# Routing tail of a top-1 mixture of experts: second expert chosen after 8 of 12 token tiles, expert units placed between the last routing steps

## The chip, the cores and the metric

One NeuronCore of one Trainium2 chip (trn2), one launch, float32 inputs and output. The metric is the device time of that launch in microseconds (us); before the change it is 557.35 us, the median of 3 runs.

## The reference, cut to what matters

```python
def _attn_ref(q, k, v, n_global, n_local):      # B, H, S, D = 2, 8, 768, 64; n_global 8, n_local 96
    scores = (1.0 / sqrt(D)) * q @ k^T
    keep = is_global | is_local                  # columns below n_global, and the last n_local before the row
    scores = where(keep, scores + bias, -1e9)    # bias: -slope(head) * distance
    return softmax(scores) @ v

def _moe_ref(x, w_gate, w_local, w1, w2):        # D, E, F = 512, 8, 1024
    logits = x @ w_gate                          # [B, S, 8]
    local_gate = sigmoid(x @ w_local)
    for b in range(B):
        for s in range(S):
            fresh_e = argmax(logits[b, s])
            e = fresh_e if s == 0 or local_gate[b, s] < 0.5 else prev_e   # else: the expert of the token before
            prev_e = e
            out[b, s] = softmax(logits[b, s])[e] * (relu(x[b, s] @ w1[e]) @ w2[e])

def _moe2_ref(x, mu_k, mu_r, w_k, w_v, w_r):     # mixes each token with the one before it
    k = relu(xk @ w_k);  v = k * k @ w_v;  r = sigmoid(xr @ w_r)
    return r * v

reference: _moe2_ref(_moe_ref(_attn_ref(q, k, v)))
```

## The kernel before, in words

The 1536 tokens (2 batches of 768) are 12 **tiles** of 128 rows. Every float32 operand of the big products is split into a high and a low part of the faster float32r format, and a product is three matmuls: high by high, low by high, high by low (`mm3`, L624 to L626).

**Attention with routing inside it.** A loop over i = 0 to 24 (`NI` is 24) does half a tile of attention (4 heads) per step: scores (L750, L754), exponentials on ScalarE (L774), transposes of the probabilities on TensorE (L785, L787), copies out of PSUM (`pt`, L794 and L796), product with v (L810). When a tile is done its output X is scaled (`route_x`, L178) and its logits are taken (`route_lg`, L192). Two tiles make a routing **group**, and a group goes through a chain of short operations that hops between engines: logits on TensorE; maximum and argmax on VectorE (L198 to L222); transposes to one row on TensorE (L232); a copy on ScalarE (`br`, L235); a scan along the row on VectorE that resolves "the expert of the token before" (L243); back to columns on TensorE (L251); one-hot on VectorE (L256); running counts on TensorE (L265 to L271); positions on VectorE (L283 to L297). Then GpSimd scatters the rows of X by expert to DRAM (`scatter`, L275); at most 3 tiles X are held. The table `plan` (filled by `at`) says in which step of the loop each link of the chain of a group is issued: its logits go to step 2 g + 4 (g is the group's second tile).

**Early expert.** After 6 tiles the counts choose the first expert (`order_a`, `order_b`, `early_pick`), its weights `wraw` (w1 in chunks 0 to 3, w2 in chunks 4 to 7, 512 KB each, 4 buffers) are loaded on SyncE's queue and split: `whi` on ScalarE (some on VectorE), `wlo` = raw minus high on GpSimd (`w_lo1`, `w_lo`), 512 or 1024 columns at a time.

**Tail.** When attention ends, the last group (tiles 10 and 11) still has its whole chain to go. Into it the kernel places **units** of the first expert's first two tiles (`fill`, `F_`): a unit is the three matmuls of one 128-row slice of the product; a tile has 16 of them (8 of w1, 8 of w2) and three sets of four transposes. `TAILF` and `RANKF` say how many units stand after each link. At the chain's end all 12 tiles' counts are known, `ranks` orders the experts, and only then the weights of the second expert are loaded. The third tile of the first expert follows, then the experts 1 to 7 in order of their counts: 256 rows each, and 80 rows more for the second (`CAPS`, `TILES`, `LAST`). If an expert has more rows than its capacity, a flag sends the kernel through `general`, which computes everything anew.

**After the experts** the rows are gathered back and the third part of the reference runs in 6 blocks of 256 tokens (L1262 to L1302).

All of it is scheduled by hand: each engine runs its instructions in the order in which the program issues them, and waits are on semaphores. Pools of buffers are released after their last reader.

## Time and profile before

| | |
|---|---|
| three timed runs | 558.14, 556.28, 557.35 us; median 557.35 |
| the profiled execution | 553.79 us, of which 551.8 us lie between first and last instruction |
| TensorE (PE) | busy 522.6 us, 95% |
| weight loads of TensorE (PEld) | busy 444.1 us, 80% |
| VectorE (DVE) | busy 349.7 us, 63% |
| ScalarE (ACT) | busy 258.4 us, 47% |
| GpSimd (POOL) | busy 117.5 us, 21% |
| mean granted clock of TensorE | 0.975 of full speed |
| chain of work that ended last | PE 74%, DVE 12%, DMA 7% |

All times of rows are counted from the start of the span. The profile gives each engine's busy time, for each idle stretch the instruction that ended it (written `[idle <-releaser]`), and the clock that TensorE was granted, as a share of its full speed; 0.50 means the lower of its two levels, 1.2 GHz, and 1.00 the upper, 2.4 GHz. Attention ends and the tail runs at about 124 to 166 us; the expert passes run to about 380 us.

### The profile page before, as it was taken

Reading aid. Unit: us, or ns where it says so; the run is one execution under the profiler, and the core shown is the slowest. Engines: PE = TensorE matmul, PEld = TensorE weight load, DVE = VectorE, ACT = ScalarE, POOL = GpSimd, SP = SyncE. Lnnn points to the kernel's source line nnn. Section 1 sums busy time; section 2 is a strip of 40 time slices with the busy share of each in tenths; the row PEclk is TensorE's granted clock in tenths of the full one; section 3 lists DMA queues with packets and bytes.
Section 4 is the critical chain, followed back from the end, with each engine's and each line's share of the span. In section 5 each row is a group of like instructions: output and inputs, shape, how many; then the busy total and the mean of one; then the engine's idle time right before and its main releaser. Section 6 shows DMA issues by size and latency. Waiting matters only on the chain.

```text
span 551.8 us, 9594 instructions
## 1 busy us (share of the span) xinstructions
PE 522.6 (95%) x3451; PEld 444.1 (80%) x3451; DVE 349.7 (63%) x760; ACT 258.4 (47%) x637; POOL 117.5 (21%) x195
## 2 busy tenths in 40 slices
PE   6999899997879899999999999999999999999995
PEld 4687777785658698889898898778898989898885
DVE  4666657686453388678998989769754444444311
ACT  2766556464214544555565655567333332424130
POOL 4101111063430000000000000053535261716130
PEclk8999999998779999999999999999999999999998
DMA  6966554554131985858889897111101010110101
GB/s 118 216 154 149 129 128 105 157 185 154 38 114 40 329 280 159 316 187 262 250 332 338 272 347 255 58 57 58 58 21 55 22 39 38 39 39 1 39 2 43
DMA packets 74279, 77.01 MB, mean 140 GB/s; under 512 B 50640, under 2 KB 50896, under 8 KB 74224
## 3 DMA queue, kind: packets, MB, share of 16 engines
q1 hardware_dynamic: 68608, 63.31, 38.0%
q0 software_dynamic: 1920, 6.29, 3.6%
q10 hardware_dynamic: 3696, 6.72, 3.4%
q8 instruction: 29, 0.48, 0.4%
q14 instruction: 26, 0.21, 0.1%
HBM read 63.30 MB, written 13.01 MB: 138 GB/s over the span
## 4 chain that ended last, share of the span: by engine, by line
PE 74%; DVE 12%; DMA 7%; issue 2%; ACT 2%; SPq 1%; POOL 0%; DVEq 0%; ACTq 0%; POOLq 0%
PE O L626 8%; PE O L624 8%; PE O L625 8%; PE S L624 7%; PE S L626 7%; PE S L625 7%; DMA wraw<-in_moe_w_dram 4%; PE PT L626 3%; PE PT L625 3%; PE PT L624 3%; PE O L810 3%; PE PT L707 2%; DVE wlo L617 2%; PE PT L785 2%; PE T L754 2%
## 5 line engine op out<-in xcount | busy, mean ns | idle before, releaser
L608 ACT ACTIVATE whi<-wraw 128x512 fp32r<-128x512 f32 x116 | 67.1, 624 | 18.6 <-DMA wraw<-in_moe_w_dram 15.2
L617 DVE TENSOR_TENSOR wlo<-wraw,whi 128x1024 fp32r<-128x1024 f32 x54 | 65.8, 1219 | 9.0 <-ACT whi L608 8.5
L1262 ACT ACTIVATE rl<-S 128x256 f32<-128x256 f32 x48 | 18.5, 385 | 80.6 <-PE S L626 80.5
L624 PE MATMUL S<-xkh,whi 128*128 128x256 f32 x192 | 54.6, 285 | 0.4 <-DVE sq L1264 0.4
L625 PE MATMUL S<-xkl,whi 128*128 128x256 f32 x192 | 53.7, 280 | 0.6 <-DVE xkl L1240 0.6
L626 PE MATMUL S<-xkh,wlo 128*128 128x256 f32 x192 | 53.7, 279 | 0.0
L1272 POOL TENSOR_TENSOR kl<-sq,kh 128x256 fp32r<-128x256 f32 x40 | 31.9, 807 | 80.5 <-ACT kh L1271 80.5
L1302 DVE TENSOR_TENSOR o<-O,sig 128x512 f32<-128x512 f32 (+1 forms) x13 | 8.5, 650 | 61.6 <-PE O L626 34.5
L1217 POOL MEMSET strip<- 128x4 f32 x2 | 0.2, 124 | 196.5 <-issue 196.5
L624 PE MATMUL O<-whi,kh 128*128 128x512 f32 (+1 forms) x104 | 39.2, 377 | 0.0
L626 PE MATMUL O<-whi,kl 128*128 128x512 f32 (+1 forms) x104 | 39.2, 377 | 0.0
L625 PE MATMUL O<-wlo,kh 128*128 128x512 f32 (+1 forms) x104 | 39.2, 377 | 0.0
L624 PE MATMUL O<-whi,hh 128*128 128x512 f32 x96 | 38.0, 396 | 0.0
L625 PE MATMUL O<-wlo,hh 128*128 128x512 f32 x96 | 37.9, 395 | 0.0
L626 PE MATMUL O<-whi,hl 128*128 128x512 f32 x96 | 37.9, 395 | 0.0
L625 PEld LDWEIGHTS S<-xkl,whi 128*128 128x128 f32 x192 | 36.1, 188 | 1.0 <-DVE xkl L1240 0.8
L624 PEld LDWEIGHTS S<-xkh,whi 128*128 128x128 f32 x192 | 36.0, 187 | 1.0 <-DVE sq L1264 0.6
L1264 DVE SCALAR_TENSOR_TENSOR sq<-S,rl 128x256 f32<-128x256 f32 x48 | 19.8, 420 | 26.0 <-ACT rl L1262 25.3
L626 PEld LDWEIGHTS S<-xkh,wlo 128*128 128x128 f32 x192 | 36.0, 188 | 0.0
L624 PE MATMUL S<-xh,whi 128*128 128x256 f32 (+1 forms) x96 | 28.0, 292 | 0.0
L624 PE MATMUL PT<-xh,whi 128*128 128x256 f32 (+1 forms) x96 | 27.9, 291 | 0.0
L796 DVE COPY pt<-PT 128x512 f32<-128x512 f32 (+1 forms) x36 | 22.3, 641 | 8.5 <-PE PT L787 7.8
(368 smaller groups left out, 1494.3 us busy)
## 6 DMA issues: line engine op xcount, KB each, us to landing
wraw<-in_moe_w_dram SPq DMA_DIRECT2D x64, 512.0 KB, 5.6
ys<-yo ACTq DMA_DIRECT2D x17, 256.0 KB, 4.8
dw<-in_moe_w_k_dram SPq DMA_DIRECT2D x8, 512.0 KB, 5.1
dw<-in_moe_w_v_dram SPq DMA_DIRECT2D x8, 512.0 KB, 4.6
xn<-xs SPq DMA_DIRECT2D x14, 256.0 KB, 4.7
vn<-in_v_dram SPq DMA_DIRECT2D x12, 256.0 KB, 4.1
kn<-in_k_dram SPq DMA_DIRECT2D x11, 256.0 KB, 5.0
qn<-in_q_dram SPq DMA_DIRECT2D x11, 256.0 KB, 5.0
```

The lines of the kernel that those rows point to most:

```text
L608: nc.scalar.activation(out=whl[r, c][0][:, sl], in_=raws[r, c][:, sl], func=ACTF.Copy)
L617: nc.vector.tensor_tensor(lo, raws.pop((r, c)), hi.bitcast(F32), op=ALU.subtract)
L624: nc.tensor.matmul(out_, lhsT=ah, rhs=bh, start=first, stop=False)
L625: nc.tensor.matmul(out_, lhsT=ah, rhs=bl, start=False, stop=False)
L626: nc.tensor.matmul(out_, lhsT=al, rhs=bh, start=False, stop=last)
L707: nc.tensor.transpose(ps[:, p * P:(p + 1) * P], src[:, 2 * p:2 * p + 2, :].rearrange("p a d -> p (a d)"), n.ident)
L754: nc.tensor.matmul(ps[a][:, b * N:(b + 1) * N], lhsT=qz[t % 2][r, 2 * g + b, :], rhs=strip[r, 2 * g + b, k0:k0 + N], start=False, stop=b == 1)
L796: nc.vector.tensor_copy(d[:, 0:ps.shape[1]], ps)
L810: nc.tensor.matmul(Os[t][a * HD:(a + 1) * HD, p * P:(p + 1) * P], lhsT=src[:, h * HD:(h + 1) * HD], rhs=d[:, (2 * c + a) * P:(2 * c + a + ...
L1262: nc.scalar.activation(out=rl, in_=ps[:, 0:TB], func=ACTF.Relu)
L1264: nc.vector.scalar_tensor_tensor(sq_, ps[:, 0:TB], 0.0, rl, op0=ALU.max, op1=ALU.mult)
L1272: (nc.gpsimd if b else nc.vector).tensor_tensor(hl, sq_, hh.bitcast(F32), op=ALU.subtract)
```

## The change

1. **Routing one step earlier.** In `plan` a group's logits go to step 2 g + 3.
2. **Second expert early.** After 8 tiles the counts are ordered a second time (tag "g"); the expert that stands fourth in them becomes expert 1 (`early_pick(rp, 3)`), and `bonus` keeps the two chosen ones at ranks 0 and 1 of the last ordering. Its w1 chunks are loaded in the tail, each as soon as a chunk of the first expert's w2 is split (`w_last`). Since its count is not the second largest, its capacity is 256, and the 80 rows more go to rank 2 (`THIRD`).
3. **Tail written anew.** Step 24 of the loop becomes straight code; the units stand one or two at a time between the links of the last group's chain, and each unit issues one piece of weight splitting (`WNEXT`).
4. **Splitting.** The first expert's w2 chunks get their `wlo` on VectorE alone, 512 columns at a time (seven of these eight halves were GpSimd's); its w1 chunks stay on GpSimd, 256 columns at a time.

```diff
-CAPS = [384, 256 + LAST] + [256] * 6
+THIRD = 2
+CAPS = [384, 256, 256 + LAST] + [256] * 5
...
-TAILF = (1, 0, 1, 1, 1, 1, 1, 1, 1)
-RANKF = (1, 2)
-X1_AT = (5, 7, 9)
-WNEXT = (1, 0, 1, 1, 2, 0, 2, 2, 1, 0, 2, 2, 0, 0, 1, 1)
+X1_AT = (5, 7)
+WNEXT = (1,) * 12 + (0,) * 4
...
-    def early_pick(self, pool):
+    def early_pick(self, pool, rank):
         nc = self.nc
-        self.fvec = self.R[:, 0:1]
+        v = self.R[:, rank:rank + 1]
+        if rank == 0:
+            self.fvec = v
+        else:
+            self.bonus = pool.tile([8, 1], F32, name="bonus")
+            nc.vector.scalar_tensor_tensor(self.bonus, self.fvec, 2.0, v, op0=ALU.mult, op1=ALU.add)
...
     def w_lo1(r, c, s):
         sl = slice(s * 512, s * 512 + 512)
         hi, lo = whl[r, c]
-        (nc.gpsimd if r == 0 else nc.vector).tensor_tensor(lo[:, sl], raws[r, c][:, sl], hi[:, sl].bitcast(F32), op=ALU.subtract)
+        if r or c >= NIN:
+            nc.vector.tensor_tensor(lo[:, sl], raws[r, c][:, sl], hi[:, sl].bitcast(F32), op=ALU.subtract)
+            return
+        for q in (0, 256):
+            sl = slice(s * 512 + q, s * 512 + q + 256)
+            nc.gpsimd.tensor_tensor(lo[:, sl], raws[r, c][:, sl], hi[:, sl].bitcast(F32), op=ALU.subtract)
...
-        split_t(xe[a], *ex, 0, n.bank("T", 1))
+        split_t(xe[a], *ex, 0, n.bank("T", 1) if a else n.bank("S", 2))
...
-        i = 2 * g[-1] + 4
+        i = 2 * g[-1] + 3
...
-        if g[-1] == 5:
-            at(i + 3, "Dm", lambda: n.order_a(rp, "f", n.cnt6, None))
-            at(i + 3, "Db", lambda: n.order_b(rp, "f"))
-            at(i + 4, "Ra", early_start)
+        if g[-1] in (5, 7):
+            e = g[-1] == 7
+            at(i + 3, "Dm", lambda e=e: n.order_a(ap2, "fg"[e], n.cnte if e else n.cnt6, n.fvec if e else None))
+            at(i + 3, "Db", lambda e=e: n.order_b(ap2, "fg"[e], rp))
+            at(i + 4, "Ra", lambda e=e: early_start(3 * e, e))
...
+        def w_last(c):
+            w_lo1(0, c, 1)
+            w_load(1, c - NIN)
+
+        wseq, w1q = [], []
         for c in range(NIN, 8):
-            wseq.append(lambda c=c: w_hi(0, c))
-            wseq.append(lambda c=c: w_lo(0, c, c < 7))
...
+            wseq += [lambda c=c: (w_hi1(0, c, 0), w_hi1(0, c, 1)), lambda c=c: w_lo1(0, c, 0), lambda c=c: w_last(c)]
...
+        early_split(0)
+        fl = fill()
+        mx, mx2, rows, scan, tn, oh, sm_, ps_ = tail
+        g = groups[-1]
+        emit_pT(NI - 1, 0)
+        emit_pT(NI - 1, 1)
+        early_row()
...
+        n.route_lg(g, g[0], xTs[g[0]])
...
+        F_(1)
+        emit_pv(NI - 1, 0)
+        emit_pv(NI - 1, 1)
+        emit_xT(g[1])
+        F_(1)
+        n.route_lg(g, g[1], xTs[g[1]])
+        mx()
+        n.turn_x(xTs[g[1]], g[1])
+        F_(2)
+        mx2()
+        n.route_x(ap, X, g[1])
+        F_(1)
+        rows()
+        F_(1)
+        scan()
+        F_(1)
+        tn()
+        oh()
+        F_(1)
+        sm_()
+        ps_()
...
+        n.order_a(rp, "r", n.cnt, n.bonus)
+        F_(2)
+        n.order_b(rp, "r", rp)
+        F_(1)
+        n.ranks(rp)
...
-    TILES = [(2,)] + [(0, 1, 2)] + [(0, 1)] * 6
+    TILES = [(2,), (0, 1), (0, 1, 2)] + [(0, 1)] * 5
```

Three places show how the change moves instructions.

**TensorE, from the last group's transposes to its scan's return** (R is the bank of the routing, S and O hold products of a unit, `hnk` is the hidden layer that is turned). Before:

```order
L232 MATMUL R_1904<-ident,ab_1887 1x128 x4
L624 MATMUL S_1820<-whi_2_1656,exexh_1807 128x512
L625 MATMUL S_1820<-wlo_2_1657,exexh_1807 128x512
L626 MATMUL S_1820<-whi_2_1656,exexl_1808 128x512
L624 MATMUL S_1820<-whi_3_1721,exexh_1807 128x512
L625 MATMUL S_1820<-wlo_3_1722,exexh_1807 128x512
L626 MATMUL S_1820<-whi_3_1721,exexl_1808 128x512
L251 MATMUL R_1925<-ones_r,er_1916 128x8 x2
```

and of the change:

```order
L232 MATMUL R_1962<-ident,ab_1926 1x128 x4
L631 MATMUL S_1957<-whi_1_1547,exexh_1838 128x512
L632 MATMUL S_1957<-wlo_1_1548,exexh_1838 128x512
L633 MATMUL S_1957<-whi_1_1547,exexl_1839 128x512
L637 MATMUL PT_1972<-ident,hnk_1892 128x128 x4
L631 MATMUL S_1957<-whi_2_1625,exexh_1838 128x512
L632 MATMUL S_1957<-wlo_2_1626,exexh_1838 128x512
L633 MATMUL S_1957<-whi_2_1625,exexl_1839 128x512
L251 MATMUL R_1991<-ones_r,er_1982 128x8 x2
```

Two units stand between the transposes and the return of the scan in both; in the changed kernel they are units 5 and 6 in place of 2 and 3, with the turning of `hnk` between them. (Units 2 to 4 have moved ahead of the transposes.)

**VectorE, around the last group's scan** (`er` is the scan, `etb` the low part of the turned hidden layer, `OH` the one-hot). Of the change:

```order
L222 SCALAR_TENSOR_TENSOR ab_1926<-fr_1952,fl_1927 128x2
L178 TENSOR_TENSOR X_1955<-PT_1932,RI 128x512
L616 TENSOR_TENSOR wlo_5_1948<-wraw_5_1623,whi_5_1947 128x512
L640 TENSOR_TENSOR etb_1895<-PT_1972,etb_1894 128x512
L616 TENSOR_TENSOR wlo_5_1948<-wraw_5_1623,whi_5_1947 128x512
L243 SCALAR_TENSOR_TENSOR er_1982<-R_1962,er_1765,br_1967 1x256
L256 TENSOR_TENSOR OH<-R_1991,iota_e 128x16
L616 TENSOR_TENSOR wlo_6_1988<-wraw_6_1716,whi_6_1987 128x512
```

Before, the scan followed `ab` directly. Now two halves of `wlo`, a copy X and one `etb` stand ahead of it, and the same kinds follow it.

**SyncE's queue, from the second tile of the first expert on** (`wraw1_c` is chunk c of expert 1, `xe1` and `x0` are rows of the first expert; TENSOR_LOAD reads an index that the routing wrote). Before:

```order
L834 DMA xe1_1869<-xs_63 128x512
L946 TENSOR_LOAD eri_2029
L946 ISA x2
L575 ISA
L575 DMA wraw1_0_2049<-in_moe_w1_dram 128x1024
L575 ISA
L575 DMA wraw1_1_2051<-in_moe_w1_dram 128x1024
L1081 TENSOR_LOAD rowi_2027
```

and of the change:

```order
L841 DMA xe1_1879<-xs_63 128x512
L577 ISA
L577 DMA wraw1_0_1941<-in_moe_w1_dram 128x1024
L577 ISA
L577 DMA wraw1_1_1980<-in_moe_w1_dram 128x1024
L577 ISA
L577 DMA wraw1_2_2028<-in_moe_w1_dram 128x1024
L1112 TENSOR_LOAD rowi_2069
```

The load of the last ordering's result (`eri`) is gone from ahead of the second expert's chunks, a third chunk joins them ahead of the row indices, and the index that they need (`fi3`) is read much earlier in the queue.

## Rows read from the trace of the kernel before

**Rows 1.** Stretches: length, busy us of PE, PEld, DVE, ACT, POOL; granted clock, DMA.
```profile
124.16:165.62 41.46, 32.02 (x186) 24.55 (x185) 23.02 (x73) 11.91 (x27) 15.55 (x11) 0.79 0.29 103
...
142.50:148.60 6.10, 5.55 (x16) 3.67 (x17) 1.90 (x6) 2.18 (x5) 0.09 (x1) 0.51 0.14 43
...
159.20:165.60 6.40, 6.35 (x24) 5.12 (x25) 2.25 (x15) 0.60 (x1) 0.00 (x0) 0.50 0.45 166
165.62:178.14 12.52, 12.52 (x61) 10.22 (x60) 4.28 (x7) 5.67 (x10) 0.00 (x0) 1.00 0.11 41
178.14:193.88 15.74, 13.72 (x70) 10.78 (x68) 6.40 (x12) 8.68 (x16) 0.00 (x0) 1.00 0.87 304
...
193.88:226.32 32.44, 32.44 (x177) 28.19 (x176) 26.46 (x62) 15.21 (x37) 0.00 (x0) 1.00 0.68 230
226.32:249.70 23.38, 23.38 (x153) 21.16 (x152) 17.40 (x43) 14.12 (x30) 0.00 (x0) 1.00 0.70 247
```

**Rows 2.** What TensorE waited for, 124.16 to 165.62: total us, times, longest.
```profile
PE R L352 <- DVE Rr L318: 3.6, 1, 3.6
PE PT L174 <- DVE eq L218: 1.9, 1, 1.9
PE R L232 <- DVE fl L209: 1.8, 1, 1.8
PE R L265 <- DVE OH L256: 1.0, 1, 1.0
PE S L624 <- ACT exexh L632: 0.7, 1, 0.7
```

**Rows 3.** What TensorE waited for, 45 to 124.16.
```profile
PE PT L785 <- DVE X L178: 1.7, 1, 1.7
PE PT L785 <- ACT peb L774: 1.2, 1, 1.2
PE PT L785 <- DVE gtf L315: 0.7, 1, 0.7
```

**Rows 4.** What VectorE waited for, 45 to 124.16, the row of X.
```profile
DVE X L178 <- DMA xs<-X,posi: 3.5, 3, 1.8
```

**Rows 5.** GpSimd in order of time: start, us, line, operation.
```profile
119.36 3.73 POOL L613 TENSOR_TENSOR wlo<-wraw,whi 128x512 fp32r<-128x512 f32 x3
...
155.61 2.35 POOL L593 TENSOR_TENSOR wlo<-wraw,whi 128x1024 fp32r<-128x1024 f32 x1
157.90 1.26 POOL L597 TENSOR_TENSOR wlo<-wraw,whi 128x512 fp32r<-128x512 f32 x1
```

**Rows 6.** VectorE in order of time, same columns.
```profile
120.63 2.49 DVE L183 TENSOR_SCALAR RI<-sm 128x8 f32<-128x8 f32 x1
...
144.64 0.74 DVE L243 TENSOR_TENSOR_SCAN er<-R,er,br 1x256 fp32r<-1x256 f32 x1 [1.08 <-ACT br L235]
...
152.04 0.68 DVE L597 TENSOR_TENSOR wlo<-wraw,whi 128x512 fp32r<-128x512 f32 x1
...
154.66 0.69 DVE L633 TENSOR_TENSOR etb<-PT,etb 128x512 fp32r<-128x512 f32 x1 [1.45 <-ACT etb L632]
...
155.51 0.15 DVE L316 TENSOR_REDUCE rkr<-gtr 8x1 f32<-8x8 f32 x1
155.69 3.50 DVE L318 TENSOR_SCALAR Rr<-iota_e,rkr 8x8 f32<-8x8 f32 x1
```

**Rows 7.** ScalarE in order of time, same columns.
```profile
150.80 0.60 ACT L632 ACTIVATE etb<-PT 128x512 fp32r<-128x512 f32 x1 [1.33 <-PE PT L630]
...
187.30 0.63 ACT L608 ACTIVATE whi<-wraw 128x512 fp32r<-128x512 f32 x1 [1.96 <-DMA wraw<-in_moe_w_dram]
```

**Rows 8.** SyncE's queue in order of time: DMA issues.
```profile
161.47 0.94 SPq L575 DMA_DIRECT2D wraw<-in_moe_w_dram  x2
...
178.34 2.85 SPq L1112 DMA_DIRECT2D xn<-xs  x3
```

**Rows 9.** The chain that ended last: one set of four transposes in a unit.
```profile
150.32 0.44 PE PT L630 x4
```

More of the change, by code (lines that the diff above doesn't have):

```diff
@@ L874, in build @@
         if g[-1] == NTT - 1:
-            tail = [[lambda: early_row()], [lgg, mx], [mx2, rows], [scan], [tn, oh], [sm_, ps_]]
+            tail = mx, mx2, rows, scan, tn, oh, sm_, ps_
             continue
@@ L935, in fill @@
                         early_split(1) if a == 0 else first_split()
-                    for _ in range(WNEXT[u]):
-                        w_next()
+                    if a == 0:
+                        for _ in range(WNEXT[u]):
+                            wseq.pop(0)()
+                    elif w1q:
+                        w1q.pop(0)()
                     yield
-        xhl0 = wp.tile([P, 2, KD, P], F32R, tag="wraw", bufs=4, name="x0s")
         def first_split():
-            split_t(x0, xhl0[:, 0], xhl0[:, 1], 0, n.bank("T", 1))
+            xhl0.append(wp.tile([P, 2, KD, P], F32R, tag="wraw", bufs=4, name="x0s"))
+            split_t(x0[0], xhl0[0][:, 0], xhl0[0][:, 1], 0, n.bank("T", 1))
+        x0, xhl0 = [], []
         def ereg(r):
@@ L1039, in build @@
                 load_vp(t + 1)
[L1040 to L1041 removed]
+            if 0 < i <= E // 2:
+                for e in (2 * i - 2, 2 * i - 1):
                     nc.scalar.dma_start(out=n.xs[e * REG:e * REG + PRE, :], in_=n.warm)
@@ L1080, in build @@
-        x0 = wp.tile([P, D], F32, tag="wraw", bufs=4, name="x0")
-        row = nc.values_load(n.rowi[:, 2, 0:1], engines=(SP,), min_val=0, max_val=E * REG - P)
-        nc.sync.dma_start(out=x0, in_=n.xs[bass.ds(row, P), :])
-        w1q = [(c, s) for c in range(2) for s in range(4)]
-        for k, _ in enumerate(fl):
-            if k > 6 and w1q:
-                c, s = w1q.pop(0)
-                if s < 2:
-                    w_hi1(1, c, s)
-                else:
-                    w_lo1(1, c, s - 2)
+        while hi_q or lo_q:
+            bg_early()
@@ new lines, in build @@
+        n.route_lg(g, g[1], xTs[g[1]])
[14 more added lines that the diff above has]
+        ps_()
+        while scq:
+            scatter(scq.pop(0))
+        n.order_a(rp, "r", n.cnt, n.bonus)
[3 more added lines that the diff above has]
+        n.ranks(rp)
+        x0.append(wp.tile([P, D], F32, tag="wraw", bufs=4, name="x0"))
@@ L1091, in build @@
+        row = nc.values_load(n.rowi[:, 2, 0:1], engines=(SP,), min_val=0, max_val=E * REG - P)
+        nc.sync.dma_start(out=x0[0], in_=n.xs[bass.ds(row, P), :])
+        for _ in fl:
+            pass
+        xhl0 = xhl0[0]
     astack.close()
@@ L1389, in build @@
                 lq.append(lambda r=r: ereg(r))
-            for c in range(0 if r > 1 else 2, 8):
+            for c in range(0 if r > 1 else 4, 8):
                 if c == 7 and r < E - 1:
```

93 lines of the change are left out of this document (32 added, 61 removed).

## The prediction

> **What bounds the kernel now.** I read the granted clock and busy time by stretch first, then what TensorE waited for in the stretches that the change touches, then VectorE, GpSimd, ScalarE and SyncE's queue in order of time beside those waits. In the expert passes TensorE has no idle time and the full clock: 32.44 us for the second expert with its three tiles, 23.38 us for one with two [rows 1]. There only TensorE's own work counts. The tail, 124.16 to 165.62, is different: of 41.46 us TensorE works 32.02 and stands idle 9.44, at a mean granted clock of 0.79 [rows 1]. The reader should see two losses there. The waits are nearly all on VectorE, the longest 3.6 us on `Rr`, the last step of the expert ordering [rows 2]; each is a link of the routing chain for which TensorE has no unit left to do. And the clock is at the lower level (0.50 and 0.51) in two stretches of about 6 us, each behind such a wait [rows 1].
>
> Two smaller losses lie outside. Between 45 and 124 us TensorE waits three times, 3.6 us together [rows 3]; VectorE in turn waited at those times for a scatter of X to land, 3.5 us in three pieces [rows 4], because X has three buffers and a tile is scattered only one step before its buffer is wanted again. And behind the tail, in the first expert's third tile, TensorE works 13.72 of 15.74 us [rows 1]: ScalarE sat in its queue at a `whi` that waited for a weight chunk until 187.30 [rows 7], and the turned hidden layer that TensorE needed stood behind it. That chunk was late since it is queued behind `xn`, issued at 178.34 [rows 8].
>
> **The change part by part.** Times are differences against the profiled execution (553.79 us, 551.8 of it span). It ran 3.6 us below the median of the runs, and I take the same difference from the median.
>
> *Routing a step earlier.* The same matmuls move to another step of the loop. A scatter then starts a whole step, some 5 us, before now, against waits of at most 1.8 us for its landing. The three waits of TensorE go: **-3.6**. Late next is VectorE itself: in the last step of the loop it has more to do than TensorE, which has no k and q to transpose there. I put **+0.5** on it (between 0 and 1).
>
> *GpSimd against VectorE.* `RI` on VectorE took 2.49 us, and ended when GpSimd's row of `wlo` ended (120.63 + 2.49 and 119.36 + 3.73, both about 123.1); `Rr` took 3.50 and ended with GpSimd's second `wlo` at 159.2 [rows 5, 6]. The short operation waits through all of GpSimd's splits that follow without a gap. The change takes the w2 splits off GpSimd, so `Rr` is free, and that is counted with the tail. The w1 splits stay, halved in width but issued in pairs, and meet steps 19 to 22 of the loop, where two ordering steps are also due. Nothing shows the price for certain: it lies between 0 (the loop's slack takes it) and 1.9, the wait of TensorE that followed `RI` [rows 2]. I take **+1.0**, the middle, since now the collision falls in steps with more VectorE work but also more of TensorE's to cover it. The Trainium skill, page "SBUF — State Buffer", section "Who interferes with whom", says that whoever starts first holds the shared port for one instruction and the other blocks. By that a waiting operation would get in after one half, which is worth 0.7 us here and would make the whole sum 541.0 in place of 541.7. The trace disagrees for these two operations: 3.50 us spans two GpSimd instructions.
>
> *The tail.* The work in it, at full clock: the two low stretches cost 5.9 us (5.55 x 0.49 + 6.35 x 0.50), and 8.7 is the most that the mean of 0.79 allows (0.21 x 41.46, idle time included); I take 7.5, so 24.5 us of work remain. To that comes the idle time of the new order. A unit is 0.70 us and a set of transposes 0.44 [rows 9]: 16 units and 3 sets make 12.52 [rows 1]. I walk along the chain:
> - The first split of the hidden chain and `early_row` share ScalarE, VectorE and the routing bank as now: 0.7, the wait that stands there now [rows 2].
> - The scan. After the last group's transposes TensorE has a unit, a set and a unit, 1.84 us. VectorE's order puts `etb` ahead of the scan, and `etb` needs the unit, the set and a ScalarE copy: 0.70 + 0.44 + 0.60 [rows 7] = 1.74. Then `etb` 0.69, a `wlo` half 0.68 and the scan 0.74 [rows 6], with some 0.2 between engines (estimate): 4.05. Idle 2.2.
> - The ordering. TensorE has one unit between `order_b` and `ranks`. VectorE still has the second `etb` to do, which waits for ScalarE: 0.60 + 0.69, then three short operations, some 0.65 (estimate from 0.15 for `rkr` [rows 6] and the gaps around it): 1.95 against 0.70. Idle 1.25.
> - Elsewhere two units and more stand before each link, against chains of some 2 us: 0.25 in all.
>
> Together 4.4 of idle time. With 0.2 for the second ordering's three tiny matmuls the tail needs 24.5 + 4.4 + 0.2 = 29.1 in place of 41.46: **-12.4**. The clock may fall once more behind the 2.2 us wait. Bounds are 0 (two waits, 2.0 us in all, in the third tile left the clock at 1.00 [rows 1]) and 3.2 (what 159.2 to 165.6 lost). I take **+0.9**, nearer to the third tile, because 2.2 is nearer to 2.0 than to 3.6.
>
> *The second expert's weights.* Now issued at 161.47, after `ranks` [rows 8]; in the changed queue they follow `xe1` and each split of w2, and three of four chunks are in long before `xn`. ScalarE has no chunk to wait for in the third tile: **-2.0** (15.74 - 13.72). Late next would be `x0`, whose load waits for the twelfth scatter and the last `wlo` half. It is wanted at unit 13 of the second tile, some 9 us after the tail's end, so it is covered; without that cover it costs a landing of some 4 us.
>
> *Costed at nothing.* Seven halves at 0.68 us [rows 6] come to VectorE, 4.8 us. It is busy 23.02 of 41.46 in the tail [rows 1], so they fit, and where they stand in a link's way they are in the idle pieces above. The 80 extra rows move from the first of the seven passes to the second; 32.44 and 23.38 change places. VectorE's 26.46 us of the long pass [rows 1] must shrink to fit 23.38: the short parts of the extra rows leave it, so some 22 remain. If this cover is gone the pass grows by a few us. The ten extra short operations of the second ordering, the moved start of the DRAM writes and the ordering of `bonus` lie beside attention.
>
> **Sum:** -3.6 + 0.5 + 1.0 - 12.4 + 0.9 - 2.0 = -15.6; 553.8 becomes 538.2 in the profile, 557.35 becomes **541.7** as the median.
>
> **The rivals.**
> - *A: the clock falls twice more.* The units between the links make four short waits in place of long ones, and each could bring the lower level. For it: the level fell now behind waits of 1.8 and 3.6 us. Against it: it stayed at 1.00 with 2.0 us of waits in the third tile [rows 1]. Price 5.9 in place of 0.9: 546.7. The Trainium skill has a rule that speaks for this and against the change: "TensorE: Matmul & The Clock Gate", section "A second HAM failure mode: psum-queue depth-cycling", tells that frequent small idles between groups of matmuls make the clock swing. The third tile does not bear it out, the tail partly does.
> - *B: the units cover the chain.* If idle time is 1.0 in place of 4.4 and neither clock nor GpSimd costs anything: 541.7 - 3.4 - 0.9 - 1.0 - 0.5 = 535.9. For it: VectorE has half the tail free. Against it: its order is fixed, and `etb` stands ahead of the scan.
> - *C: slower.* The place is the tail, the mechanism is the lower clock through all of it, fed by routing that waits behind the units' own splits. Then 24.5 us of work take 49, with 4.4 idle 53.6 in place of 41.46: +12.1 where I have -12.4 + 0.9, so 541.7 + 23.6 = 565.3. It decides against the change from about 33 us at the lower level on. Against it: no row shows that level for more than some 6 us at a time.
> - *D: given back downstream.* If VectorE or the weight loads bound the passes and not TensorE, the gain would turn into waits there: 557. Against it: TensorE has no idle time in any of the passes, with DMA at 0.70 [rows 1].
> - *E: the change doesn't do what it says.* An expert above its capacity raises the flag, and everything is computed anew, far slower. The reference, worked through for its default seed, gives after 8 tiles the counts 252, 116, 107, 106, 92, 112, 39, 200 and after 12 the counts 324, 177, 166, 172, 115, 206, 96, 280. The fourth at 8 tiles is the sixth expert (112), which ends with 206, below 256; rank 2 gets 280, below 336. So the flag stays down.
>
> **How the numbers follow.** Forecast 0.55 (its own range 538 to 546), A 0.20, B 0.13, C 0.04, D 0.05, E 0.03. The range takes in A and B with the bounds of their costs, 535 to 549.5, and leaves C, D and E outside. A difference under 0.3% cannot be told from none here: only D is there, 0.05. Slower are C and E, 0.07; faster 0.88.
>
> **What would show it.** Right: no wait on X between 45 and 124 us; in the tail no VectorE operation of 2 us or more, and TensorE's longest waits at the return of the scan (about 2.2) and at `ranks` (about 1.25); the tail, from the same transposes on, about 29 us long at a granted clock above 0.9; `wraw` of the second expert issued before `rowi` is read, and no wait in the third tile; expert passes of 23.4 and 32.4 us in this order. Wrong: a granted clock near 0.8 in the tail (A or C), VectorE operations stretched to 1.3 us or more in the loop's last steps with TensorE waiting behind them (the GpSimd cost too low), or idle time in the first two-tile pass (D).

## The result, and the profile after

The changed kernel takes 539.3 us (median of 4 runs, 536.34 to 541.43) against 556.82 us for the kernel before in the same series (554.13 to 558.14): a ratio of 0.969, 95% interval 0.963 to 0.975. Forecast were 541.7 and a range of 535 to 549.5. The profiled execution took 539.79 us, its span is 537.6 where it was 551.8.

The page's busy times of the kernel after: TensorE has nearly as much to do as before (522.6 us), in a shorter span.

```profile
PE 518.4 (96%) x3455; PEld 441.7 (82%) x3455; DVE 347.2 (65%) x775; ACT 259.0 (48%) x638; POOL 110.6 (21%) x199
```

The stretches of the kernel after, in the columns of [rows 1]: the tail (from the same transposes on to the first expert's second tile), the part of it with a low clock, the first expert's third tile, the first pass (two tiles) and the second (three).

```profile
121.39:152.04 30.65, 27.07 (x182) 21.63 (x181) 18.39 (x68) 11.81 (x27) 4.34 (x5) 0.89 0.33 114
138.90:145.80 6.90, 6.69 (x28) 5.34 (x28) 2.73 (x12) 0.60 (x1) 0.97 (x1) 0.54 0.39 126
...
164.52:178.18 13.66, 13.15 (x66) 10.55 (x64) 6.35 (x11) 8.13 (x15) 0.00 (x0) 1.00 0.78 268
178.18:203.78 25.60, 23.92 (x157) 21.50 (x156) 24.75 (x50) 14.22 (x29) 0.00 (x0) 1.00 0.79 280
203.78:236.73 32.95, 32.95 (x180) 28.46 (x178) 20.04 (x57) 16.02 (x38) 0.00 (x0) 1.00 0.57 200
```

The tail answers to the first row of [rows 1]: 30.65 us in place of 41.46, with 3.58 us idle in place of 9.44. The row of the first pass (from 178.18) is the surprise: a pass of two tiles that takes 25.60 us, with VectorE busy nearly all the time.

All that TensorE waited for from 45 to 205 us, the view of [rows 2] and [rows 3] in one answer:

```profile
PE R L251 <- DVE er L243: 2.1, 1, 2.1
PE R L1152 <- DVE xl L1158: 1.7, 1, 1.7
PE R L354 <- DVE Rr L318: 0.7, 1, 0.7
PE R L192 <- DVE erow L344: 0.7, 1, 0.7
PE O L633 <- DVE ehl L640: 0.5, 1, 0.5
PE R L232 <- DVE ab L222: 0.4, 1, 0.4
```

The waits on X are gone; at the scan's return (`er`), at the ranks (`Rr`) and at `early_row` (`erow`) it stands idle where the prediction put idle time. The wait on `xl` is new. It lies in the first pass, where the next expert's third row tile is to be turned into a bank that VectorE has not yet read.

VectorE in order of time, the rows that answer to [rows 6] and those of the new wait, and GpSimd's, to [rows 5]:

```profile
111.34 0.24 DVE L318 TENSOR_SCALAR Rg<-iota_e,rkg 8x8 f32<-8x8 f32 x1
...
137.03 0.69 DVE L640 TENSOR_TENSOR etb<-PT,etb 128x512 fp32r<-128x512 f32 x1 [1.06 <-ACT etb L639]
137.64 0.68 DVE L616 TENSOR_TENSOR wlo<-wraw,whi 128x512 fp32r<-128x512 f32 x1
138.24 0.73 DVE L243 TENSOR_TENSOR_SCAN er<-R,er,br 1x256 fp32r<-1x256 f32 x1
...
147.47 0.22 DVE L318 TENSOR_SCALAR Rr<-iota_e,rkr 8x8 f32<-8x8 f32 x1
...
186.89 0.42 DVE L1177 SCALAR_TENSOR_TENSOR hl<-PT,hh 128x256 fp32r<-128x256 f32 x1 [0.51 <-ACT hh L1176]
187.23 0.68 DVE L1158 TENSOR_TENSOR xl<-R,xh 128x512 fp32r<-128x512 f32 x1
```

```profile
110.81 7.13 POOL L620 TENSOR_TENSOR wlo<-wraw,whi 128x256 fp32r<-128x256 f32 x10
```

The scan comes late exactly as forecast: `etb`, a `wlo` half, then `er`. `Rr` takes 0.22 us, not 3.50. And `Rg`, the same operation in the new second ordering, takes 0.24 us in the middle of ten narrow GpSimd operations.

ScalarE in the first pass, beside it SyncE's queue, the view of [rows 7] and [rows 8]:

```profile
185.43 1.15 ACT L610 ACTIVATE whi<-wraw 128x512 fp32r<-128x512 f32 x2 [1.78 <-DMA wraw<-in_moe_w_dram]
186.49 0.36 ACT L1176 ACTIVATE hh<-PT 128x256 fp32r<-128x256 f32 x1
```

```profile
134.12 10.43 SPq L577 DMA_DIRECT2D wraw<-in_moe_w_dram  x3
...
175.69 2.60 SPq L1138 DMA_DIRECT2D xn<-xs  x3
...
180.98 0.38 SPq L579 DMA_DIRECT2D wraw<-in_moe_w_dram  x1
```

The second expert's first chunks are issued from 134 us on, before the row index. Its last chunk is issued at 180.98 behind the rows of the next expert, and ScalarE waits for it until 185.43 with the hidden layer's `hh` behind it. VectorE's `hl` waits for that `hh`, and `xl`, for which TensorE waits, stands behind `hl`. The jam that stood in the third tile before has moved one pass on.

Where TensorE starts each stage, for the two profiled executions and for a second one of the changed kernel (run e12 below), gives the lengths in us; the last column but one is from the last stage on, "passes" are the two first expert passes together:

| | start of tail | tail | second tile | third tile | passes | next four | last expert | last stage | span |
|---|---|---|---|---|---|---|---|---|---|
| before | 124.16 | 41.46 | 12.52 | 15.74 | 56.36 | 93.54 | 26.90 | 181.12 | 551.8 |
| after | 121.39 | 30.65 | 12.48 | 13.66 | 58.55 | 93.55 | 26.25 | 181.07 | 537.6 |
| after (e12) | 121.19 | 27.95 | 12.49 | 13.65 | 61.03 | 93.55 | 27.43 | 180.91 | 538.2 |

### The profile page after: what moved, and what is told of

It is laid out like the page before. It is cut to its first block, busy times and chain, and to the rows that moved or that the text cites. A ratio compares the mean times of both kernels' runs of the same rounds, so it can differ in the third digit from the quotient of the medians.

```text
span 537.6 us, 9632 instructions
## 1 busy us (share of the span) xinstructions
PE 518.4 (96%) x3455; PEld 441.7 (82%) x3455; DVE 347.2 (65%) x775; ACT 259.0 (48%) x638; POOL 110.6 (21%) x199
## 4 chain that ended last, share of the span: by engine, by line
PE 85%; DVE 7%; DMA 4%; ACT 2%; issue 1%; POOL 0%; SPq 0%; POOLq 0%; DVEq 0%; ACTq 0%
PE O L631 9%; PE O L633 9%; PE O L632 9%; PE S L631 7%; PE S L633 7%; PE S L632 7%; PE O L817 4%; PE PT L631 4%; PE PT L633 4%; PE PT L632 4%; PE PT L792 2%; PE PT L714 2%; PE S L761 2%; PE R L192 2%; PE T L761 2%; PE PT L794 1%
## 5 line engine op out<-in xcount | busy, mean ns | idle before, releaser
L610 ACT ACTIVATE whi<-wraw 128x512 fp32r<-128x512 f32 x124 | 71.5, 624 | 12.2 <-DMA wraw<-in_moe_w_dram 8.7
L633 PE MATMUL PT<-xh,wlo 128*128 128x256 f32 (+1 forms) x96 | 27.5, 286 | 0.0
```

Source lines behind the costliest of these rows:

```text
L610: nc.scalar.activation(out=whl[r, c][0][:, sl], in_=raws[r, c][:, sl], func=ACTF.Copy)
L633: nc.tensor.matmul(out_, lhsT=al, rhs=bh, start=False, stop=last)
```

## The experiments

Times of runs are medians; "the change" is the changed kernel, at 539.3 and, on the chip of the last runs, 539.74 us. The kernel before took 554 to 556 us beside these runs.

### What a VectorE operation pays beside GpSimd

**e4: GpSimd's splits 512 columns wide again.**

```diff
-        for q in (0, 256):
-            sl = slice(s * 512 + q, s * 512 + q + 256)
-            nc.gpsimd.tensor_tensor(lo[:, sl], ...)
+        nc.gpsimd.tensor_tensor(lo[:, sl], ...)
```

> The changed kernel with GpSimd's low parts of w1 512 columns at a time, as before, in place of two halves of 256. It measures what a VectorE operation pays beside GpSimd. Theory R (it waits for the one GpSimd instruction that runs): short VectorE operations beside GpSimd, at 104 to 121 us, last 0.2 to 1.5 us, up to 1.25 us longer than alone, and never longer than one GpSimd instruction of 1.25; the time is 0 to 1.5 us above the changed kernel. Theory S (it waits through all GpSimd instructions that follow without a gap, as the prediction read RI and Rr): operations of 2 us and more are there beside runs of two or three, TensorE waits 1 to 2 us more before 122 us, and the time is 1 to 2.5 us above.

Measured: 548.73 us (544.8 to 551.91), ratio 0.987 (0.979 to 0.994) to the kernel before: some 9 us of the gain are gone. The profiled execution is the longest of the four. VectorE, GpSimd, TensorE's waits from 98 to 130 us and a stretch of e4:

```profile
111.18 0.15 DVE L316 TENSOR_REDUCE rkg<-gtg 8x1 f32<-8x8 f32 x1
111.36 3.20 DVE L318 TENSOR_SCALAR Rg<-iota_e,rkg 8x8 f32<-8x8 f32 x1
```

```profile
110.82 3.71 POOL L618 TENSOR_TENSOR wlo<-wraw,whi 128x512 fp32r<-128x512 f32 x3
```

```profile
PE R L329 <- DVE Rg L318: 2.7, 1, 2.7
```

```profile
114.60:127.90 13.30, 13.28 (x66) 10.86 (x66) 6.55 (x21) 1.96 (x8) 2.69 (x3) 0.50 0.38 113
```

`Rg` starts at the same time as in the change, and ends at 114.56, just when the run of three wide operations ends (110.82 + 3.71 = 114.53). TensorE waits 2.7 us for it, and then works 13.3 us at the lower of its two levels. The tail starts at 129.66, 8.3 us later than in the change: 2.3 us more of waiting, and 5.9 us more for the same work. Theory S has the mechanism, but priced it at 1 to 2.5 us: it left the clock out.

In the change, a VectorE operation gets in between two halves. `RI` there, and the first of the two halves beside it:

```profile
107.99 0.47 DVE L183 TENSOR_SCALAR RI<-sm 128x8 f32<-128x8 f32 x1
```

```profile
107.69 0.74 POOL L620 TENSOR_TENSOR wlo<-wraw,whi 128x256 fp32r<-128x256 f32 x1
```

`RI` ends at 108.46, just behind this half (108.43), while the second half, which began at 108.37, runs on. `Rg` ends at 111.58, just behind the first of its ten (110.81 + 0.74 = 111.55). The price of the halves is small: ten take 7.13 us, where the five whole splits of e4 take 3.71 + 2.49.

The Trainium skill, page "SBUF — State Buffer", section "Who interferes with whom", says that the engine that issues first gets the shared pair for the whole instruction, and that the other blocks. Read so, a blocked operation gets in after one instruction of the other engine. Beside the narrow operations the rows agree; beside the wide ones they do not, as 3.20 us is longer than any one GpSimd operation there (1.24). The same page of the Trainium skill also says that `tensor_reduce` never contends and `tensor_scalar` can; `rkg` (0.15 us inside the run) and `Rg` agree with that.

**e9: the kernel before, with GpSimd's splits of w2 256 columns wide.**

```diff
-            nc.gpsimd.tensor_tensor(lo, raw, hi.bitcast(F32), op=ALU.subtract)
...
+        for q in range(4):
+            sl = slice(q * 256, q * 256 + 256)
+            if pool_lo or q > 1:
+                nc.gpsimd.tensor_tensor(lo[:, sl], raw[:, sl], hi[:, sl].bitcast(F32), op=ALU.subtract)
...
```

> The kernel before with GpSimd's low parts of w2 in pieces of 256 columns, on the same engine and in the same places. It asks whether it is the width of GpSimd's instructions or the length of its run that a VectorE operation waits for. Theory N (VectorE gets in between two narrow instructions, as seen in the changed kernel beside ten halves of w1): Rr takes 1.0 us or less in place of 3.50, TensorE's wait for it 1.3 or less, and the stretch at the lower clock behind it shrinks or goes; the tail is 35 to 39 us in place of 41.46, the time 2 to 5 us below the kernel before. Theory S (the whole run counts, whatever the width): Rr takes 3 to 4 us again, tail 41 to 42, time within 1 us of the kernel before.

Measured: 551.46 us (9 runs), ratio 0.994 (0.991 to 0.997).

```profile
159.52 0.76 DVE L318 TENSOR_SCALAR Rr<-iota_e,rkr 8x8 f32<-8x8 f32 x1
```

```profile
156.08 4.17 POOL L595 TENSOR_TENSOR wlo<-wraw,whi 128x256 fp32r<-128x256 f32 x6
```

```profile
123.63:163.93 40.30, 35.04 (x187) 27.23 (x185) 18.59 (x72) 12.02 (x27) 16.94 (x21) 0.70 0.21 68
```

This one decides nothing. `Rr` is short, but it started late, and it too ended with the run (160.28 and 160.25). The tail is 40.30 us, outside both the 35 to 39 of theory N and the 41 to 42 of theory S: the wait of 3.55 us is down to 0.8, yet the granted clock in this tail is 0.70, lower than before's 0.79. The median, 3.0 us below that of the kernel before beside it, would fit theory N. The evidence for the width is `RI` and `Rg` in the change and `Rg` in e4.

### The two parts that shorten the tail, each alone

**e6: the kernel before, with w2's low parts all on VectorE.**

```diff
-            for s, eng in ((0, nc.vector), (1, nc.gpsimd)):
...
+        for s in range(2):
+            sl = slice(s * 512, s * 512 + 512)
+            nc.vector.tensor_tensor(lo[:, sl], raw[:, sl], hi[:, sl].bitcast(F32), op=ALU.subtract)
```

(for the chunks, too, that GpSimd had whole)

> The kernel before with all low parts of the first expert's w2 on VectorE in halves of 512 columns, none on GpSimd. Theory (Rr took 3.50 us because of GpSimd's two operations, and the clock fell behind TensorE's wait for it): Rr takes 0.2 to 0.3 us, TensorE's wait at the ranks falls from 3.55 to about 0.5, the lower clock at 159 to 165 us goes with it (3.2 us), and VectorE's 4.8 us more cost 0 to 2: the tail is 34.8 to 36.8 in place of 41.46, the time 4.7 to 6.7 us below the kernel before. Rival (the time was bound by the chain and the clock falls anyhow): the stretch at the lower clock is still there, gain 3 us or less.

Measured: 550.09 us, ratio 0.987 (0.979 to 0.995). `Rr`, the tail, its end, and the third tile:

```profile
154.35 0.22 DVE L318 TENSOR_SCALAR Rr<-iota_e,rkr 8x8 f32<-8x8 f32 x1
```

```profile
123.49:158.86 35.37, 29.07 (x187) 22.40 (x185) 21.64 (x80) 11.90 (x27) 7.29 (x7) 0.86 0.28 92
150.00:158.86 8.86, 7.70 (x46) 5.91 (x44) 6.57 (x27) 2.51 (x5) 1.36 (x2) 1.00 0.20 68
171.32:189.59 18.27, 15.02 (x69) 11.79 (x68) 7.75 (x13) 8.67 (x16) 0.00 (x0) 0.92 0.81 282
```

`Rr` takes 0.22 us in place of 3.50. The tail is 6.1 us shorter, as the theory had it, and its end runs at the full clock. But the third tile takes 18.27 us in place of 15.74: 2.5 us are given back. ScalarE's longest wait on a weight chunk there is 3.2 us, where it was 2.0 before: the second expert's chunks are still loaded behind the ranks, and the tail no longer hides it.

**e7: the kernel before, with routing one step earlier.**

```diff
-        i = 2 * g[-1] + 4
+        i = 2 * g[-1] + 3
```

(with the DRAM writes moved as in the change, and `early_row` in step 24)

> The kernel before with routing one step of the loop earlier, nothing else (the starting writes to DRAM move with it, and the first ordering's row is read a link earlier). Theory: the waits on X and the scatters between 45 and 124 us go, TensorE's last group of attention starts 2 to 3.6 us earlier, the tail stays 41.5: the time is 2 to 3.6 us below the kernel before. Rival (a short VectorE operation that now falls beside GpSimd's runs of 512 columns waits for the whole run and the clock falls behind it, as Rg did at 111.36 for 3.20 us in the changed kernel with wide splits): one VectorE operation of 2 us or more between 95 and 124 us with TensorE behind it, and the time is the same or up to 6 us above.

Measured: 547.55 us, ratio 0.986 (0.982 to 0.990), about 7 us, twice what the theory had. TensorE's two longest waits from the tail's start to the second expert's pass, and its tail and third tile:

```profile
PE R L352 <- DVE Rr L318: 3.9, 1, 3.9
PE O L624 <- ACT ehh L632: 1.9, 1, 1.9
```

```profile
120.54:155.57 35.03, 27.76 (x183) 21.36 (x182) 20.28 (x62) 11.25 (x26) 12.57 (x9) 0.90 0.21 69
168.07:186.93 18.86, 15.70 (x69) 12.31 (x68) 8.35 (x14) 8.67 (x16) 0.00 (x0) 0.86 0.80 273
```

The tail starts 3.6 us earlier, the size forecast. It is also 6.4 us shorter, which the theory did not have: the last but one group has left the tail, and with it the waits on `eq` and `OH` of [rows 2]. `Rr` still costs 3.9 us, and again the third tile grows, by 3.1 us, with ScalarE 3.1 us at a chunk. So each of the two parts takes some 6 us off the tail, and each alone gives 2.5 to 3 back in the third tile. Of that, 1.2 and 1.1 us are more waiting, the rest is TensorE's work at a lower clock (0.92 and 0.86). The tail written anew (part 3 of the change) was not run alone: e6 and e7 together take 12.5 us off the tail, the change 10.8 and 13.5, which leaves little for it, but no run shows its share.

**e5: the change, with the second expert's loads where they were before.**

```diff
-            w_load(1, c - NIN)
...
         n.ranks(rp)
+        for c in range(2):
+            w_load(1, c)
```

(the later chunks and the order of their splits as before)

> The changed kernel without the early loads: expert 1 is still chosen after 8 tiles, but its w1 chunks are loaded where the kernel before loads them, two behind the ranks and the rest behind the tail. Theory (the prediction's -2.0): TensorE waits about 2 us again in the third tile, which takes 15.7 us in place of 13.66, and the tail itself stays as it is; the median is 541.3 or, since the first two-tile pass waits for later chunks too, up to 544. Rival (the loads were no limit; the third tile got shorter because VectorE and ScalarE came free): third tile within 0.5 us of 13.66, median within 1 us of 539.3.

Measured: 541.59 us, ratio 0.979 (0.973 to 0.984). The third tile:

```profile
162.96:177.83 14.87, 13.41 (x65) 10.47 (x64) 6.35 (x11) 8.46 (x15) 0.00 (x0) 1.00 0.85 314
```

14.87 us lies between the two theories' values (15.7 and about 13.7): loading early is worth 1.2 of the 2.1 us that the third tile gained, and some 2 us of the median, though the runs of both kernels overlap (540.68 to 544.98, and 536.34 to 541.43).

### Where the new wait in the first pass comes from

**e2: the last chunk ahead of the next expert's rows. e3: five of VectorE's decoding operations moved to the next pass.**

```diff
# e2
-                if c == 7 and r < E - 1:
+                if c == 7 and 1 < r < E - 1:
                     lq.append(lambda r=r: x_load(r + 1))
                 lq.append(lambda r=r, c=c: w_load(r, c))
+                if c == 7 and r == 1:
+                    lq.append(lambda r=r: x_load(r + 1))
# e3
-                B_(BL1[f])
+                B_(0 if r == 1 and f < 6 else BL1[f] + (r == 2 and f < 5))
```

> The changed kernel with expert 1's last weight chunk issued ahead of the three row loads of expert 2, not behind them. It tells apart two causes of the new 1.7 us wait of TensorE on xl in the first two-tile pass. Theory L (the late chunk: ScalarE stood 1.78 us at whi with the relu copy of the hidden layer behind it): ScalarE does not wait there and TensorE's wait falls to 0.3 or less, median near 537.6. Theory V (VectorE has more work than fits: it is busy 24.27 of the pass's 25.12 us): ScalarE's wait goes but TensorE still waits 1.0 to 1.7 us for xl, median 538 to 539.5.

> The changed kernel with five of the decoding operations that VectorE does in the background (about 0.6 us each, 3 us together) moved from the first two-tile pass to the three-tile pass behind it, where VectorE is busy 19.5 of 32.4 us. Theory V: xl comes earlier, the 1.7 us wait of TensorE in the first two-tile pass goes although ScalarE still waits for the chunk, median near 537.6. Theory L: the wait stays at 1.2 us or more since VectorE itself waits for ScalarE's copy, median 538.8 or more. In both the three-tile pass stays at 32.4.

Measured: e2 540.42 us, e3 542.3 us, neither faster than the change. TensorE's waits from 152 us on, of e2 and of e3:

```profile
PE R L1152 <- DMA xn<-xs: 2.6, 1, 2.6
```

```profile
PE R L1152 <- DVE xl L1158: 2.3, 1, 2.3
PE R L410 <- DVE dj L405: 1.0, 1, 1.0
```

VectorE in e3, ahead of that `xl`:

```profile
185.77 0.42 DVE L1177 SCALAR_TENSOR_TENSOR hl<-PT,hh 128x256 fp32r<-128x256 f32 x1 [2.95 <-ACT hh L1176]
```

In e2 ScalarE hardly waits for the chunk any more (0.7 us in all), but then the rows come late, and the first of the next expert's transposes wait 2.6 us for them. In e3 the wait stays although VectorE has less to do, because now VectorE itself waits 2.95 us for `hh`, and the moved work makes a new wait. So VectorE's load alone is not the cause. It has a part: in the change VectorE waited only 0.51 us for `hh` (1.45 in e12) and was at work for the rest of TensorE's 1.7 us (2.7). Of chunk and rows one was late in each of these runs, and what matters is what stands behind the late one in an engine's order.

**e1: the scan ahead of `etb`.**

```diff
         rows()
-        F_(1)
         scan()
         F_(1)
+        F_(1)
         tn()
```

> The changed kernel with the last scan issued directly behind the four transposes that feed it, so that on VectorE it stands ahead of etb and of the second wlo half; TensorE's order is the same. Theory (the 2.06 us wait comes from VectorE's order, and the fall of the clock from 139 to 146 us comes from that wait): TensorE waits under 0.3 us at the scan's return, the clock stays at its upper level through the tail, which gives back about 3.2 us; the wait at ranks grows from 0.72 to about 1.3 because the units are faster. Tail 121.39 to the second tile: 30.65 - 2.0 - 3.2 + 0.6 = about 26 us, the median near 534.7. Rival (the clock falls without that wait, by the run of small matmuls of the links): the lower level is there again for some 7 us, the tail is 28.6, the median near 537.3. Second rival (another link of the chain is late, such as the copy of the row on ScalarE): a wait of 1 us or more remains at the scan's return and the time moves by less than 1 us.

Measured: 537.96 us, ratio 0.969 (0.962 to 0.976), the change's own. TensorE's longest wait from 121 to 200 us, and the tail and the first pass:

```profile
PE R L1152 <- DVE xl L1158: 3.4, 1, 3.4
```

```profile
121.29:147.60 26.31, 24.37 (x182) 19.34 (x181) 18.39 (x68) 11.81 (x27) 4.55 (x5) 1.00 0.39 131
173.74:202.47 28.73, 25.36 (x157) 22.94 (x156) 24.56 (x48) 14.22 (x29) 0.00 (x0) 0.94 0.72 254
```

The wait at the scan's return is gone, the tail is at its full clock and 4.3 us shorter, as forecast. And 3.1 us of it come back in the first pass: the pass takes 28.73 us in place of 25.60, the wait on `xl` is 3.4 us, and the clock falls behind it (0.94 in the pass). So the median stays above the 534.7 of the theory. How much of the 4.3 us is the scan, e12 shows.

**e12: the change once more.**

> The changed kernel once more, as it is, on the same chip as the run before, for the comparison of the two. Both theories: its median within 0.5% of 539.3; where the granted clock is 0.99 or more, no or a shorter stretch at the lower clock behind the scan's return and a time near 536, where it is 0.985 a time near 540.

Measured: 539.74 us (6 runs, 537.56 to 541.48), ratio 0.972 (0.969 to 0.976). The runs at a mean clock of 0.990 to 0.993 took 537.56 to 541.48 us, that at 0.985 539.79: the mean clock does not sort them. The tail, the place that was slow in the first profile, and the first pass:

```profile
121.19:149.14 27.95, 24.15 (x182) 19.41 (x181) 18.41 (x68) 11.83 (x27) 4.54 (x5) 1.00 0.35 124
138.90:145.80 6.90, 5.94 (x42) 4.63 (x43) 4.82 (x20) 2.23 (x4) 1.70 (x2) 1.00 0.55 188
...
175.28:203.37 28.09, 25.37 (x158) 22.99 (x156) 24.35 (x48) 14.24 (x29) 0.00 (x0) 0.94 0.74 256
```

The same program with the same wait of 2.1 us at the scan, and no low clock behind it. So e1's theory that this wait makes the clock fall is not borne out; the scan's share in e1 is 27.95 - 26.31 = 1.6 us. And here too the shorter tail is paid for in the first pass: the pass takes 28.09 us, its wait on `xl` is 2.7 us, the clock falls behind that, and tail and passes together take 88.98 us where the first profile has 89.20.

### A version that keeps the gain

**e8: scan first, the last ordering one unit earlier, the first w2 chunk ahead of the rows, and in the first pass the late chunk's splits and the row transposes one or two units later.**

```diff
-        F_(2)
+        F_(1)
         n.order_b(rp, "r", rp)
-        F_(1)
+        F_(2)
         n.ranks(rp)
...
+                lq.append(lambda r=r: w_load(r, 4))
                 lq.append(lambda r=r: x_load(r))
...
-                W_((1, 2, 2, 1, 1, 1, 1, 1)[f])
+                W_(((1, 2, 0, 0, 2, 2, 2, 2) if d else (1, 2, 2, 1, 1, 1, 1, 1))[f])
```

(`d` is 1 in the first pass, and `x_hi` and `x_lo` stand `d` units later; the scan as in e1)

> The changed kernel with four moves: the scan directly behind its transposes (as before), the last ordering's matmul one unit earlier, expert 1's first w2 chunk loaded ahead of its rows, and in the first two-tile pass the splits of the late chunk and the transposes of the next expert's rows one to two units later. Theory (the late chunk in ScalarE's order is what gave 1.7 to 3.4 us back in that pass): no wait of TensorE over 0.6 us between 128 us and the three-tile pass, upper clock throughout, the first two-tile pass 24 us in place of 25.6 and 28.7; the span is 537.6 - 4.4 - 0.9 - 1.7 = about 530.6, the median 532 to 533. Rival (the loads themselves are the limit, by their rate): a wait of 2 us or more turns up elsewhere in that pass or the next, on a later chunk, and the median is 536 or more.

Measured: 537.84 us, ratio 0.969 (0.965 to 0.973). The profiled execution, 542.58 us, is the longest of the five. In it the two passes take 56.88 us, without a wait; but in the third tile TensorE waits 1.4 us for rows that now stand behind that chunk, and the last expert takes 34.39 us in place of 26.25, with waits of 5.3 us in all (on `yg` 2.0, `ehl` 1.8, `hn` 1.5) and a granted clock of 0.90. ScalarE there:

```profile
346.69 0.63 ACT L610 ACTIVATE whi<-w 128x512 fp32r<-128x512 f32 x1 [6.57 <-PE S L633]
...
348.21 0.60 ACT L649 ACTIVATE hn<-S 128x512 f32<-128x512 f32 x1 [0.40 <-DVE wlo L616]
```

**e10: e8 without 18 of the last stage's 20 weight loads.**

```diff
+        if len(dwk) == 2:
+            dw[i] = dwk[i % 2]
+            return
```

> The kernel of the run before with the scan first and the loads moved, but 18 of the 20 loads of the last stage's weights (512 KB each, 9.4 MB) are left out and the first two pieces decoded again in their place, so that the last stage works with other weights; every instruction of the engines is as it was. Theory (the rate of the loads is the next bound, so that what the tail gains comes back as waits on late chunks further on): no wait of ScalarE on a chunk over 1 us after 180 us, TensorE's waits in the last expert, 5.3 us there, fall to 1.5 or less, the median is 532 to 534. Rival (the order of VectorE's and ScalarE's background work is the bound there): TensorE's waits in the last expert stay within 1.5 us of 5.3 and the median at 536.5 or more.

Measured: 539.74 us, ratio 0.975 (0.972 to 0.978). ScalarE's longest wait on a chunk is down from 3.9 to 1.4 us, so the loads were crowded; but TensorE's waits in the last expert, 2.4 us on `yg` and 1.5 on `hn`, are 3.9 together, and the time is no better. The rival holds: it is not the rate of the loads that costs the time here. ScalarE's row of e8 points at the order: a `whi` of the last stage waits 6.57 us for TensorE to free its buffer, and `hn`, for which TensorE waits, is behind it. The edit of e8 had 11 pieces of splitting in the pass where the change has 10, so every later piece came one place too early.

**e11: e8 with 10 pieces, and the rows ahead of the last stage's first piece.**

```diff
-                W_(((1, 2, 0, 0, 2, 2, 2, 2) if d else (1, 2, 2, 1, 1, 1, 1, 1))[f])
+                W_(((1, 2, 0, 0, 2, 2, 2, 1) if d else (1, 2, 2, 1, 1, 1, 1, 1))[f])
...
-        pump(1)
+        pump(2)
         dec_load(PIECES[0])
-        pump(1)
         dec_load(PIECES[1])
```

> The kernel of the run with the scan first and the loads moved, with two corrections: the first two-tile pass issues 10 pieces of splitting, as the changed kernel does, and not 11, and expert 1's rows are loaded ahead of the first piece of the last stage's weights. Theory P (the losses in the last expert came from the splits running one piece ahead of the program, so that a whi of the last stage stood in ScalarE's order ahead of hn): from the second expert on ScalarE's order is that of the changed kernel, the last expert's first row turn to its end takes 26.3 us as there, no wait of TensorE over 1 us between 128 and 360 us, the span is 530 to 532 and the median 532 to 534, 1% below the changed kernel on the same chip. Rival D (the loads' rate is the bound): waits on chunks in the last expert, 2 us or more in all, median 536 or more.

Measured: **533.67 us** (6 runs, 533.06 to 536.25), ratio 0.963 (0.959 to 0.967), beside e12's 0.972 (0.969 to 0.976) on the same chip: 1.1% faster than the change, 3.7% faster than before. The tail, a part of it with a low clock, and the first pass:

```profile
120.89:148.56 27.67, 25.88 (x182) 20.37 (x181) 18.41 (x68) 11.83 (x27) 4.34 (x5) 0.94 0.36 125
140.00:146.00 6.00, 5.42 (x26) 4.16 (x27) 3.53 (x16) 1.63 (x3) 1.94 (x2) 0.72 0.58 218
174.79:198.72 23.93, 23.93 (x157) 21.50 (x156) 23.26 (x47) 13.81 (x28) 0.00 (x0) 1.00 0.83 291
```

No wait over 1.04 us remains between 128 and 360 us, and the last expert takes 27.11 us (theory P: 26.3). The first pass is 23.93 us with VectorE still busy 23.26 of it: full, but with nothing late in its way. ScalarE still waits 7.2 us in all for chunks between 300 and 353 us, the longest 3.3, so the sign of rival D is there; but TensorE waits for little behind it, and the median is the one of theory P. The two corrections were made together, so their shares are not known.

## Why the prediction was right, and which steps were off

The forecast came true in sign and size, 2.4 us from the median. In the two profiles of the change the span fell by 14.2 and 13.6 us, where the sum said 15.6. Step by step, from the table above:

| step | forecast | profile | e12 |
|---|---|---|---|
| routing earlier, VectorE bound, GpSimd (start of tail) | -2.1 | -2.77 | -2.97 |
| tail with clock | -11.5 | -10.81 | -13.51 |
| second tile | 0 | -0.04 | -0.03 |
| second expert's weights (third tile) | -2.0 | -2.08 | -2.09 |
| passes, "costed at nothing" | 0 | +2.19 | +4.67 |
| the rest | 0 | -0.69 | +0.33 |
| sum | -15.6 | -14.20 | -13.60 |

For the tail before, the prediction named two stretches at the lower clock. There is a third, behind waits of 1.0 (`OH`) and 0.7 us (`exexh`):

```profile
134.80:138.20 3.40, 3.40 (x24) 2.70 (x24) 1.19 (x9) 0.60 (x1) 0.98 (x1) 0.51 0.22 82
```

- **Routing a step earlier** was right as costed: the waits on X are gone and the tail starts 2.8 us earlier. VectorE did not become the bound in the loop's last step: where +0.5 was put, one wait of 0.42 us is left, on `ab`. What the step also does, by e7, is to shorten the tail; the prediction had that inside the tail's sum and did not see that it comes from here.
- **GpSimd, +1.0,** was too much for the change as it is: that wait of 0.42 us is the only one left in the loop, and e7, without the halves, has it too (0.5). The step that failed is the reading "the short operation waits through all of GpSimd's splits that follow without a gap". It holds for splits of 512 columns (`Rr`, and `Rg` in e4), not for the halves: `RI` and `Rg` got in between them. And the bounds, 0 to 1.9, were far too narrow for the case that the reading described: with wide splits the collision would have fallen on `Rg` and cost 8.3 us of the loop, clock included. The halving, which the prediction called a change of width, is worth some 9 us.
- **The tail.** The work of 24.5 us was right: e12's TensorE is busy 24.15 us at full clock. The third low stretch cost 1.7 us, which with the 5.9 of the other two makes 7.6; the 7.5 that was chosen between 5.9 and 8.7 came near this without the row, which is luck. Idle time was 3.6 to 3.8, where 4.4 was forecast: 2.06 of 2.2 at the scan, for the reason given; 0.7 of 0.7 at `early_row`; 0.7 to 0.95 of 1.25 at the ranks. The clock, +0.9 between bounds of 0 and 3.2, was 2.9 in one profile (27.07 busy against 24.15) and 0 in the other. A value between the two was fair; that it would be one number was not.
- **The second expert's weights** came out at the forecast 2.0, but by luck. The prediction took away all of the 2.02 us of waiting; 0.51 of it is still there, on `ehl`. The missing part was made up by 0.57 us of work that left the third tile (13.72 to 13.15 us), since the transposes of the 80 rows more now stand in the first pass. By e5 the early loading is worth 1.2.
- **"Costed at nothing"** is the step that failed with the other sign. The prediction let the two passes change places, put VectorE at some 22 us in the two-tile pass, and said that the pass grows by a few us if this cover is gone. Its 23.38 us for that pass is a misreading, as its window ends before the pass does: 56.36 - 32.44 = 23.92. VectorE is busy 24.75 of 25.60 us and TensorE waits 1.7 to 2.7 us on `xl`; another 0.5 us of the +2.19 are the transposes that came from the third tile. What the prediction did not name is what is late next: the last w2 chunk, with ScalarE's `hh` queued behind it. It had found this very jam in the third tile of the kernel before and took it as solved. The shorter the tail, the longer this wait: 1.7, 2.7 and 3.4 us for tails of 30.65, 27.95 (e12) and 26.31 us (e1).
- **Rivals.** Of A there was one stretch at the lower level in the tail at most. B's premise, that the units cover the chain with 1.0 us of idle time, was wrong in the change (3.6) and nearer in e1 (1.94). C did not come, but e4 is its mechanism in the loop. D came true in part, with the sign that the prediction gave for it, idle time in the first two-tile pass: that pass took 1.7 us more than its 23.92 in the first profile, with the clock at 1.00, and 4.2 us more in e12, with the clock at 0.94. The flag stayed down.

## What to carry to other kernels

When a stretch gets shorter, go through the next one for what was loaded just in time for the old length: here a late chunk, ahead of a VectorE with little to spare, took back 1.7 to 4.8 us (the lower clock behind the wait included) in the change, e12 and e1. Between engines with fixed orders a late transfer costs what stands behind its first reader, so move the reader back and not only the transfer forward, and keep the number of background pieces per stage, or all later stages shift. Where two engines block each other, cut the operations of the one off the critical path narrower: the cheap edit here was the width of GpSimd's splits.

## What the runs showed of the hardware that was not expected

- A `tensor_scalar` of 8 x 8 on VectorE took 0.24 us beside ten GpSimd operations of 256 columns, and 3.20 us at the same place beside three of 512 columns, ending with the last of them. Beside the narrow ones it got in after one of them. Why the width decides stays open, and e9 does not tell.
- The granted clock is no function of the program's waits alone. Behind the same wait of 2.1 us at the scan the lower level lasted 6.9 us in one execution of the change and was absent in another; the two tails differ by 2.7 us. In e11 it came behind a wait of only 0.8 us (0.72 at 140 to 146 us). What decides is not in these rows.
